# Batch 1's query pairs 2 and 3 transposed by DMA, and the third quarter of the output weights loaded earlier

## The chip, the cores and the metric

The kernel runs on one core of a Trainium2 chip. A core has a matrix engine (PE, with its weight loads listed apart as PEld), a vector engine (DVE), a scalar engine (ACT), a general engine (POOL), a queue engine that issues transfers (SP), and 16 DMA engines. Each engine runs its own instructions in order and waits on semaphores for the others. The metric is the device time in microseconds (us); lower is better. All times below are us unless they are marked ns.

## The reference

Two stages follow each other: a linear attention over 8 batches of 8 heads, 576 tokens and 64 channels a head, and a gated MLP whose input is the attention's output with the heads side by side (4608 tokens by 512 channels).

```python
q_s = exp(q - max(q)); q_s = q_s / sum(q_s, axis=-1)      # softmax of q over the channels
k_s = exp(k - max(k)); k_s = k_s / sum(k_s, axis=2)       # softmax of k over the tokens
kv  = einsum('bhsd,bhse->bhde', k_s, v)                   # 64 x 64 for each head
x   = einsum('bhsd,bhde->bhse', q_s, kv)                  # attention output, 4608 x 512 in all
h   = x @ w_in                                            # 512 -> 2048
out = (h * sigmoid(beta * h)) @ w_out                     # 2048 -> 512, float32
```

## The kernel before

**Tiles.** The tokens are worked off in nine slabs of 512 columns: slab t (0 to 7) holds the first 512 tokens of batch t, slab 8 the last 64 tokens of all eight batches. The heads go in four pairs `hp`, a pair filling 128 rows. For a slab, *pass 1* multiplies the slab's `XT` with `WIN` into `GT` (16 tiles `f` of 128 features, four products each) and ACT applies the gate; *pass 2* multiplies `GT` with `WOUT` (16 features by four token groups `u`, 64 products) into four PSUM banks, which are copied to `O2S` and stored.

**What a batch needs before its slab.** `load_swapped` brings q into `QF` in four pieces `x` (256 KB each): piece 0 has pair 0, piece 1 pair 2, and pieces 2 and 3 together pairs 1 and 3. `load_k` and `load_v` bring `KF` and `VF`. `exp_q` (L309, instruction L314, on ACT) makes `EQ`; `norm_main` (L331) normalises it: a row sum (L338) and a reciprocal (L339) on DVE, and a product (L340) on DVE or POOL. The normalised `EQ` must be turned so that the channels lie on the rows, into `QT`. There are two ways: `t_steps` (L375) turns 128 x 128 blocks on PE against an identity (L370, PSUM) and copies them out with one instruction for a group of pairs (L391), and `t_dma` (L396) lets a transfer, issued on SP, do it (L401). `exp_kc` (L318, instruction L322) makes `EK` on ACT, `cast_v` (L352, instruction L357) makes `VB`. `kv_half` multiplies `VB` and `EK` of two pairs on PE and normalises the result on DVE into `KVC` (L441, L443); `out_half` multiplies `QT` and `KVC` and copies the result to `XT` (L459), one pair by ACT and one by DVE.

**The order of the work** is written out by hand: the program is one list of operations, each engine gets its own in list order, and waits follow from the tiles that are read and written. Transfers are nearly all issued on SP, also in list order, so one that has to wait holds back those that stand behind it. What batch 1 needs is put between the products of slab 0's pass 2: the function `tick` counts products (the count starts at 64 there, as pass 1 of slab 0 stands ahead), and a list `todo` (L754) says at which count which steps of batch 1 are put in. Pairs 0 and 1 go first (`kv_half(1, (7, 0), 0)`, `out_half(1, (1, 2), 0)`), pairs 2 and 3 follow after pass 2 (L814, L817), between the first products of slab 1's pass 1 (`by_m`).

**Weights.** `w_out` comes in five loads (`load_wout`, L550) into staging tiles that `w_in` used before: features 0 to 3, 4 to 7, 8 to 11 (1 MB each), 12 and 13, then 14 and 15 one by one. `scale_wout` (L560, instruction L562 on DVE) multiplies each feature's 128 x 512 by 1/beta and writes `WOUT`; pass 2 needs feature f's `WOUT` for its products 4f+1 to 4f+4, except that for the last two features the order is by halves of the token groups. In the list the load of features 8 to 11 stands behind q's pieces 0, 2 and 3 of batch 1, and the loads of batch 2 (`load(2)`) stand ahead of all of these DVE and ACT steps.

Of the kernel before, what the change touches and what calls it, by code (L numbers as in the profile page):

```python
# [163 lines left out]
def bass_efficient_attn_shen__then__act_swish_beta_kernel(  # L164
# [12 lines left out]
    with ExitStack() as es:  # L177
# [94 lines left out]
        def load_swapped(b, xs=range(4)):  # L272
            i = b % 2
            for x in xs:
                s0, d0, n = SLOTS[x]
                a = bass.AP(qt_h, (b * H + s0) * S * D,
                            [[4 * D, 128], [n * S * D, 2], [1, 4 * D]])
                o = bass.AP(QF[i], d0 * 4 * D, [[H * 4 * D, 128], [n * 4 * D, 2], [1, 4 * D]])
                add(SP, lambda e, o=o, a=a: e.dma_start(o, a),
                    w=[("qf", i, hp, x) for hp in ((0,), (2,), (1, 3), (1, 3))[x]],  # L280
                    slot=f"qs{i}{x}")
# [70 lines left out]
        def cast_v(b, hp, eng=POOL, part=None):  # L352
            i = b % 2
            j0, n = ((0, NG), (0, 5), (5, 4))[0 if part is None else part + 1]
            o = bass.AP(VB[i], (hp * NG + j0) * VW, [[NHP * NG * VW, 128], [VW, n], [1, 64]])
            a = bass.AP(VF[i], hp * KW + j0 * D, [[NHP * KW, 128], [64, n], [1, 64]])
            add(eng, lambda e: (e.copy if eng == ACTE else e.tensor_copy)(o, a),  # L357
                r=[("vf", i, hp), ("vone", i)],
                w=[("vb", i, hp, h) for h in ((0, 1) if part is None else (part,))])
# [15 lines left out]
        def t_steps(b, hps, pool=MB, eng=DVE):  # L375
            i = b % 2
            st = {}

            def one(n, hp, j):
                if n == 0 and j == 0:  # L380
                    st["b"] = bank(pool)
                p = PS[st["b"]]
                pb = p[:, :].bitcast(BF16)
                c = n * 512 + j * 128
                mm(pb[:, c:c + 128], bass.AP(EQ[i], hp * 512 + j * 128, [[2048, 128], [1, 128]]),
                   IDB[:, :], True, True, r=[("eq", i, hp), "idb"], w=[("ps", st["b"])],
                   bk=st["b"], tr=True)
                if n == len(hps) - 1 and j == 3:
                    w = len(hps) * 512
                    o = bass.AP(QT[i], hps[0] * 512, [[2048, 128], [1, w]])  # L390
                    add(eng, lambda e: (e.copy if eng == ACTE else e.tensor_copy)(o, pb[:, 0:w]),  # L391
                        r=[("ps", st["b"])], w=[("qt", i, h) for h in hps], bank=[st["b"]])
            return [lambda n=n, hp=hp, j=j: one(n, hp, j) for n, hp in enumerate(hps)
                    for j in range(4)]
# [146 lines left out]
        def go(steps):  # L541
            for s in steps:
                s()
# [16 lines left out]
        def scale_wout(f, n=4):  # L560
            for f in range(f, f + n):
                add(DVE, lambda e, f=f: e.tensor_scalar(  # L562
                    WOUT[:, f, :], STAGE[f // 4][:, f % 4, :], RB[:, f:f + 1], None, ALU.mult),
                    r=[SKEY[f // 4][f % 4], "rb"], w=[("wout", f)])
# [122 lines left out]
                at(m)  # L687
        load_wout(0)
        load_wout(4)
        load_swapped(1, (0, 2, 3))  # L690
        load_wout(8)
        load_swapped(1, (1,))
        load_k(1, 4, (0, 1))
        load_wout(12, 2)
        load_v(1, 4, (0, 1))
# [51 lines left out]
        for t in range(NSLAB):  # L747
            todo = []
            if t == 0:
                def evacs():  # L750
                    o2_evac(0, 0, 3, DVE)
                    o2_evac(0, 1, 4, ACTE)

                todo = [(104, lambda: go(t_steps(1, (0, 1), (1,), ACTE))),  # L754
                        (104.1, lambda: cast_v(1, 0, ACTE)),
                        (111, lambda: go(t_steps(1, (2, 3), (2,), ACTE))),
                        (111.1, lambda: (scale_wout(14, 2), exp_kc(1, 2), exp_kc(1, 3))),
                        (116, lambda: kv_half(1, (7, 0), 0)),
                        (122, lambda: out_half(1, (1, 2), 0)), (124.5, evacs)]
            elif t == 1:  # L760
                todo = [(103, lambda: (kv_prods(2, (1, 2), (0, 2)), kv_evac(2, (1, 2)))),
                        (118, lambda: block(2))]
            elif t < 7:
                todo = [(104, lambda: block(t + 1))]
            todo = sorted(todo, key=lambda x: -x[0])
            slot = [0]

            def tick():
                slot[0] += 1
                while todo and todo[-1][0] <= slot[0]:  # L770
                    todo.pop()[1]()

            if 2 <= t < 7:
                if t < 5:
                    load(t + 2 if t == 2 else t + 3)
                for hp in (0, 2):
                    norm_main(t + 1, hp, 2)
                    t_dma(t + 1, hp, 2)
                if t in (2, 3, 4, 6):
                    norm_rem(t // 2 if t != 3 else 0)  # L780
                    tr_dma(t // 2 if t != 3 else 0)
                if t == 2:
                    load(5)
            elif t == 1:
                for hp in range(NHP):
                    cast_v(2, hp)
            if t < 2:
                slot[0] = NM * FIRST[t]
            for f in range(FIRST[t] if t < 2 else 0, NF):
                pass1_tile(t, f, tick)  # L790
            if t == 0:
                load(2)
                scale_wout(0)
                scale_wout(4)
                exp_q(1, (0, 1, 3, 2))
                norm_main(1, 0, 1, POOL)
                norm_main(1, 1, 1, POOL)
                norm_main(1, 3, 1, POOL)
                scale_wout(8)
                norm_main(1, 2, 1, POOL)  # L800
                exp_kc(1, 0, 2)
                scale_wout(12, 2)
                for hp in range(1, NHP):
                    cast_v(1, hp)
                pass2_group(0, (0, 1, 2, 3), (3, 4, 5, 6), tick)
                while todo:
                    todo.pop()[1]()
                at = by_m(1, 0, FIRST[1])
                o2_evac(0, 2, 5, ACTE)
                o2_evac(0, 3, 6, DVE)  # L810
                add(ACTE, lambda e: e.activation(DUMMY[:, 2:3], WARM[:, 0:1], ACT.Silu),
                    r=["warm"], w=["dummy"])
                at(0, 0, 3)
                kv_half(1, (7, 0), 2)  # L814
                at(1, 0, 3)
                at(0, 3, 5)
                out_half(1, (7, 7, 7, 0), 2)  # L817
                at(0, 5)
                at(1, 3)
                at(2)  # L820
                at(3)
                store(0)
                load(3)
                load_qrem(0)
                continue
            nb = [t + 2] if t + 2 < B else []
            if t == 1:
                nb = [2, 3]
            late = []
            for b in nb:  # L830
                if t == 1 and b == 2:
                    exp_q(2)
                    for hp in range(2):
                        norm_main(2, hp, 1, POOL)
                    t_dma(2, 0, 2)
                for hp in (0, 2):
                    exp_kc(b, hp, 2)
                if b > 2:
                    late.append(b)
                if b > 3:  # L840
                    for hp in range(NHP):
                        cast_v(b, hp)
            for b in late:
                exp_q(b)
                if b % 2 == 1:
                    exp_qr(b // 2)
                if b == 3:
                    exp_qr(0)
            for u in range(4):
                if (t, u) == (8, 3):  # L850
                    last_tile(u, ((0, 384), (384, 512)), (OB[orot[0] % 2], MB[0]))
                    continue
                pass2_group(t, (u,), (OB[orot[0] % 2],), tick)
                orot[0] += 1
                if t == 1 and u == 0:
                    for hp in range(2, 4):
                        norm_main(2, hp, 1, POOL if hp == 2 else DVE)
                    t_dma(2, 2, 2)
                    for hp in range(NHP):
                        cast_v(3, hp)  # L860
            while todo:
                todo.pop()[1]()
            if t < 8:
                store(t)
# [30 lines left out]
```

The softmax here doesn't subtract the row's maximum and nothing guards it: scores larger than these inputs give would overflow.

## Time and profile before

| | |
|---|---|
| median of 9 runs | 280.04 us (279.42 to 281.3) |
| the profiled execution | 279.77 us, its span 278.0 us |
| PE busy | 273.0 us, 98% of the span |
| ACT, DVE, POOL busy | 166.5, 103.0 and 35.2 us |
| DMA, mean rate | 180 GB/s, 50.12 MB in all |
| granted TensorE clock | 1.0 over the whole span |

The page gives one execution's span from its first to its last instruction; the time that is measured is 1.77 us longer (279.77 against 278.0). A group line of the page names the source line, the engine, the operation and the tiles (written <- read), how many there were, their busy time and the mean of one, and behind the bar how long the engine had been idle just before them, and who ended that. A line of the timeline gives the start, the length, the engine and queue (SPq is SP's issuing), the source line and how many instructions were drawn together. Matrix products overlap: the next one starts 0.216 us after the last while one is listed as 0.379 us long, so a run of n products reads n x 0.216 plus 0.16.

### The profile page before, as it was taken

The page shows a single profiled execution, that of the slowest core. Times are in us where ns is not written, and L with a number is a line of the kernel's source. Part 1 is how long each engine was busy: PE and PEld are TensorE (multiplying, and loading weights), DVE is VectorE, ACT ScalarE, POOL GpSimd, SP SyncE. Part 2 cuts the span into 40 slices and gives each one's busy share as a digit, 9 for nine tenths or more (in the row PEclk, how much of TensorE's full clock was granted, in tenths as well). Part 3 has the DMA queues.
Part 4 walks back from the last instruction along what each step waited for, and adds up shares of the span by engine and source line. Part 5 has one row for each costly group of instructions (what it writes and reads, how often), then busy time and mean ns, then how long its engine had stood idle before and what let it go on. Part 6 is the DMA issues. An engine that isn't in the chain of part 4 may idle for free.

```text
span 278.0 us, 4625 instructions
## 1 busy us (share of the span) xinstructions
PE 273.0 (98%) x1929; PEld 131.4 (47%) x1929; DVE 103.0 (37%) x204; ACT 166.5 (60%) x240; POOL 35.2 (13%) x52
## 2 busy tenths in 40 slices
PE   7999999999999999999999999999999999999995
PEld 3545444444445454545454545444444444444443
DVE  4744785007580149115720562035603200110012
ACT  5768666899578736793579447953741275027500
POOL 2630341308000305030003000000000000000000
PEclk9999999999999999999999999999999999999999
DMA  7999999999099998950599133002500110011022
GB/s 234 381 387 401 386 390 374 400 377 152 6 324 338 232 358 258 388 109 2 170 387 201 21 151 75 2 4 110 136 0 2 75 75 2 0 81 70 2 74 77
DMA packets 42173, 50.12 MB, mean 180 GB/s; under 512 B 21028, under 2 KB 29476, under 8 KB 41000
## 3 DMA queue, kind: packets, MB, share of 16 engines
q1 hardware_dynamic: 41312, 48.90, 55.0%
q10 hardware_dynamic: 840, 0.93, 1.0%
q8 instruction: 15, 0.25, 0.4%
q14 instruction: 6, 0.05, 0.1%
HBM read 36.71 MB, written 9.44 MB: 166 GB/s over the span
## 4 chain that ended last, share of the span: by engine, by line
PE 86%; DMA 8%; SPq 4%; DVE 1%; issue 0%
PE PS L372 86%; DMA O2S<-in_moe_w_out_dram 4%; DMA O2S<-in_moe_w_in_dram 4%; SPq L569 2%; SPq L250 1%; DVE WOUT L562 1%; SPq L293 0%; PE PS L370 0%; SPq L298 0%; DVE O2S L724 0%
## 5 line engine op out<-in xcount | busy, mean ns | idle before, releaser
L648 ACT ACTIVATE GT<-PS,BETA 128x512 bf16<-128x512 f32 x144 | 96.4, 690 | 61.5 <-PE PS L372 61.4
L372 PE MATMUL PS<-WOUT,GT 128*128 128x512 bf16 (+2 forms) x592 | 128.0, 374 | 0.1
L372 PE MATMUL PS<-XT,WIN 128*128 128x512 bf16 x576 | 126.3, 379 | 0.0
L372 PEld LDWEIGHTS PS<-XT,WIN 128*128 128x128 bf16 x576 | 60.4, 105 | 63.3 <-issue 0.7
L372 PEld LDWEIGHTS PS<-WOUT,GT 128*128 128x128 bf16 x592 | 56.4, 98 | 66.5 <-DVE WOUT L562 1.1
L703 DVE COPY O2S<-PS 128x512 f32<-128x512 f32 x33 | 22.7, 688 | 124.6 <-PE PS L372 124.5
L357 POOL CAST VB<-VF 128x576 bf16<-128x576 f32 x29 | 20.7, 714 | 85.3 <-DMA VF<-in_v_dram 84.1
L338 DVE TENSOR_REDUCE QS<-EQ 128x8 f32<-128x512 bf16 (+1 forms) x22 | 20.1, 912 | 17.6 <-ACT EQ L314 17.6
L459 ACT CAST XT<-PS 128x512 bf16<-128x512 f32 x14 | 7.6, 587 | 23.1 <-PE PS L372 23.1
L322 ACT ACTIVATE EK<-KF 128x1152 bf16<-128x1152 f32 (+1 forms) x19 | 18.4, 1005 | 4.1 <-DMA KF<-in_k_dram 3.9
L314 ACT ACTIVATE EQ<-QF 128x512 bf16<-128x512 f32 x32 | 17.7, 616 | 3.1 <-DMA QF<-in_q_dram 3.1
L340 DVE TENSOR_TENSOR EQ<-EQ,QI 128x1024 bf16<-128x1024 bf16 (+1 forms) x12 | 14.3, 1192 | 0.4
L340 POOL TENSOR_TENSOR EQ<-EQ,QI 128x512 bf16<-128x512 bf16 x10 | 10.5, 1048 | 30.4 <-DVE QI L339 30.1
L459 DVE CAST XT<-PS 128x512 bf16<-128x512 f32 x14 | 9.1, 686 | 12.8 <-PE PS L372 12.8
L372 PEld LDWEIGHTS PS<-VB,EK 64*64 64x64 bf16 x576 | 6.5, 107 | 4.5 <-issue 2.5
L372 PE MATMUL PS<-VB,EK 64*64 64x65 bf16 x576 | 7.9, 193 | 0.3 <-POOL VB L357 0.3
L648 ACT ACT_TABLE_LOAD x5 | 6.4, 1283 | 0.1
L372 PE MATMUL PS<-XT 128*128 128x512 f32 x6 | 5.0, 1009 | 1.5 <-DVE XT L226 1.5
L372 PE MATMUL PS<-QT,KVC 64*64 64x512 bf16 x64 | 6.2, 384 | 0.1
L562 DVE TENSOR_SCALAR WOUT<-O2S,RB 128x512 bf16<-128x512 f32 x8 | 5.3, 703 | 0.8 <-DMA O2S<-in_moe_w_out_dram 0.6
L339 DVE RECIPROCAL QI<-QS 128x8 f32<-128x8 f32 (+1 forms) x22 | 5.0, 226 | 0.8
L322 ACT ACT_TABLE_LOAD x4 | 5.1, 1283 | 0.1
(51 smaller groups left out, 68.6 us busy)
## 6 DMA issues: line engine op xcount, KB each, us to landing
out_dram<-O2S SPq DMA_DIRECT2D x8, 1024.0 KB, 4.5
QF<-in_q_dram SPq DMA_DIRECT2D x30, 256.0 KB, 5.9
KF<-in_k_dram SPq DMA_DIRECT2D x6, 1152.0 KB, 8.3
VF<-in_v_dram SPq DMA_DIRECT2D x6, 1152.0 KB, 11.3
KF<-in_k_dram SPq DMA_DIRECT2D x8, 288.0 KB, 8.2
VF<-in_v_dram SPq DMA_DIRECT2D x8, 288.0 KB, 8.5
WST<-in_moe_w_in_dram SPq DMA_DIRECT2D x8, 256.0 KB, 7.5
O2S<-in_moe_w_in_dram SPq DMA_DIRECT2D x4, 512.0 KB, 11.0
```

Source lines behind the costliest of these rows:

```text
L314: add(ACTE, lambda e, o=o, a=a: e.activation(o, a, ACT.Exp), r=[("qf", i, hp, x) for x in ((2, 3) if hp % 2 else (hp // 2,))], w=[("eq", i ...
L322: add(ACTE, lambda e: e.activation(o, a, ACT.Exp), r=[("kf", i, h) for h in range(hp, hp + n)], w=[("ekc", i, h) for h in range(hp, hp + n)])
L338: add(DVE, lambda e: e.tensor_reduce(s_, a, AX.X, ALU.add), r=ks, w=[("qs", i, hp0)])
L339: add(DVE, lambda e: e.reciprocal(v_, s_), r=[("qs", i, hp0)], w=[("qi", i, hp0)])
L340: add(eng, lambda e: e.tensor_tensor(a, a, vb, ALU.mult), r=ks + [("qi", i, hp0)], w=ks)
L357: add(eng, lambda e: (e.copy if eng == ACTE else e.tensor_copy)(o, a), r=[("vf", i, hp), ("vone", i)], w=[("vb", i, hp, h) for h in ((0, 1 ...
L372: add(PE, lambda e: e.matmul(o, l, r_, start=start, stop=stop, tile_position=tp), r=r, w=w, bank=[bk])
L459: add(eng, lambda e, eng=eng, bk=bk, hp=hp: (e.copy if eng == ACTE else e.tensor_copy)(XT[i][:, hp, :], PS[bk][:, :]), r=[("ps", bk)], w=[ ...
L562: add(DVE, lambda e, f=f: e.tensor_scalar(WOUT[:, f, :], STAGE[f // 4][:, f % 4, :], RB[:, f:f + 1], None, ALU.mult), r=[SKEY[f // 4][f % ...
L569: add(SP, lambda e: e.dma_start(STAGE[c][:, m:m + nm, :], a), w=SKEY[c][m:m + nm], slot=f"win{c}{m}")
L648: add(ACTE, lambda e: e.activation(GT[:, f, :], PS[bk][:, :], ACT.Silu, scale=BETA[:, f:f + 1]), r=[("ps", bk), "beta"], w=[("gt", f)], ba ...
L703: add(eng, lambda e: (e.copy if eng == ACTE else e.tensor_copy)(O2S[t % 2][:, u, :], PS[bk][:, :]), r=[("ps", bk)], w=[("o2", t % 2, u)], ...
```

## The change

Four things are moved in the list, all of them for slab 0's pass 2.

1. q's piece 3 of batch 1 is loaded behind the 1 MB of output weights 8 to 11, not ahead of it.
2. On DVE the four `scale_wout(8)` stand ahead of the normalisation of pairs 1 and 3, not behind it; the normalisation of pair 2 stands behind features 12 and 13, and its product is done by DVE, not by POOL.
3. Pairs 2 and 3 of batch 1 are turned by `t_dma`, not on PE: eight PE turns and one ACT copy go, one SP transfer comes. It stands on SP behind the last of batch 1's values, and `load(2)` stands behind it.
4. The PE turns of pairs 0 and 1 stand three products later (count 107, not 104); `exp_kc` of pairs 2 and 3 stands at count 119.1, not 111.1, with the same neighbours on ACT.

```diff
         load_wout(0)
         load_wout(4)
-        load_swapped(1, (0, 2, 3))
+        load_swapped(1, (0, 2))
         load_wout(8)
-        load_swapped(1, (1,))
+        load_swapped(1, (3, 1))
         load_k(1, 4, (0, 1))
...
-                todo = [(104, lambda: go(t_steps(1, (0, 1), (1,), ACTE))),
-                        (104.1, lambda: cast_v(1, 0, ACTE)),
-                        (111, lambda: go(t_steps(1, (2, 3), (2,), ACTE))),
-                        (111.1, lambda: (scale_wout(14, 2), exp_kc(1, 2), exp_kc(1, 3))),
+                todo = [(107, lambda: go(t_steps(1, (0, 1), (1,), ACTE))),
+                        (107.1, lambda: cast_v(1, 0, ACTE)),
+                        (111.1, lambda: scale_wout(14, 2)), (119.1, lambda: (exp_kc(1, 2), exp_kc(1, 3))),
                         (116, lambda: kv_half(1, (7, 0), 0)),
                         (122, lambda: out_half(1, (1, 2), 0)), (124.5, evacs)]
...
             if t == 0:
-                load(2)
                 scale_wout(0)
                 scale_wout(4)
                 exp_q(1, (0, 1, 3, 2))
                 norm_main(1, 0, 1, POOL)
+                scale_wout(8)
                 norm_main(1, 1, 1, POOL)
                 norm_main(1, 3, 1, POOL)
-                scale_wout(8)
-                norm_main(1, 2, 1, POOL)
                 exp_kc(1, 0, 2)
                 scale_wout(12, 2)
+                norm_main(1, 2, 1)
+                t_dma(1, 2, 2)
+                load(2)
                 for hp in range(1, NHP):
                     cast_v(1, hp)
```

## The prediction

> **What bounds the kernel now.** I read the page's busy line and its chain first, then the chain in order of time, then each engine's timeline around slab 0's pass 2 (28 to 47 us), last DMA from 33 to 72 us.
>
> ```profile
> PE 273.0 (98%) x1929; PEld 131.4 (47%) x1929; DVE 103.0 (37%) x204; ACT 166.5 (60%) x240; POOL 35.2 (13%) x52
> ```
> ```profile
> 22.63 11.78 DMA O2S<-in_moe_w_out_dram
> 34.40 0.03 issue
> 34.43 1.79 DVE WOUT L562 x2
> 36.22 0.05 issue
> 36.27 1.04 PE PS L372 x4
> 37.30 0.45 PE PS L370 x8
> 37.75 1.51 PE PS L372 x7
> 39.26 0.45 PE PS L370 x8
> 39.71 235.30 PE PS L372 x1667
> ```
>
> PE is the bound: from 39.71 on the chain is PE alone, to 275 us. Ahead of that it runs through the load of weights 8 to 11 (lands 34.40) and two scalings. So what PE loses or saves before 39.71 moves the end one for one, unless a later wait eats it, and a new PE wait anywhere is paid in full.
>
> ```profile
> 29.81 1.67 DVE L562 TENSOR_SCALAR WOUT<-WST,RB 128x512 bf16<-128x512 f32 x4 [1.02 <-DMA WST<-in_moe_w_out_dram]
> 34.43 2.58 DVE L562 TENSOR_SCALAR WOUT<-O2S,RB 128x512 bf16<-128x512 f32 x4
> 37.93 1.77 DVE L562 TENSOR_SCALAR WOUT<-O2S,RB 128x512 bf16<-128x512 f32 x2
> 40.79 0.49 DVE L562 TENSOR_SCALAR WOUT<-O2S,RB 128x512 bf16<-128x512 f32 x1 [0.19 <-DMA O2S<-in_moe_w_out_dram]
> 41.78 0.23 DVE L443 TENSOR_TENSOR KVC<-PS,RC 128x64 bf16<-128x64 f32 x1
> ```
> ```profile
> 33.70 2.22 POOL L340 TENSOR_TENSOR EQ<-EQ,QI 128x512 bf16<-128x512 bf16 x2 [0.27 <-DVE QI L339]
> 39.48 0.74 POOL L357 CAST VB<-VF 128x576 bf16<-128x576 f32 x1 [0.46 <-DMA VF<-in_v_dram]
> ```
> ```profile
> 28.07 9.24 PE L372 MATMUL PS<-WOUT,GT 128*128 128x512 bf16 x40
> ```
>
> Four scalings take 1.67 alone but 2.58 beside POOL's products; two take 1.77 beside one. PE's 40 products need 40 x 0.216 + 0.16 = 8.80 and take 9.24: 0.44 is waiting for those scalings.
>
> **The change, part by part.**
>
> *Weights 8 to 11.* One 256 KB piece of q no longer stands ahead: at the 374 GB/s of that slice 0.70, so they land at 33.70, not 34.40 (the issue stays at 22.63, as it waits there for its staging tile). The four scalings run 33.73 to 35.40 with POOL idle (its product of pair 0 is over at 33.44). PE wants feature 8 at 28.07 + 32 x 0.216 = 34.98 and feature 9 at 35.84: both are ready. Saved: 0.44.
>
> *PE turns of pairs 2 and 3.* Eight turns take 0.45 of PE's order (39.26 to 39.71). Saved: 0.45, together 0.89. The ACT copy (1.01) goes as well; ACT has idle time there and this is worth nothing.
>
> *What is late next, POOL.* `kv_half` needs `VB` of pair 1, whose values land at 39.43; POOL's cast ends at 40.22, unchanged. PE would come to it at 28.07 + 52 x 0.216 + 0.45 = 39.75 and waits to about 40.27; today it starts at 40.72. The 0.89 is capped at 0.45.
>
> *What is late next, DVE.* q's piece 3 lands at 33.70 + 0.70 = 34.40, so ACT's pair 1 (0.63 each) is done at 35.11 and pair 3 at 35.63; pair 2 is unchanged. DVE then does pair 1's sum and reciprocal (0.69 + 0.20, with 0.03 between) after the scalings: 35.32 to 36.2, pair 3's to 37.0. POOL's products (1.04 each) run 36.37 to 37.41 and 37.49 to 38.53. PE turns pair 1 at 28.07 + 43 x 0.216 + 0.22 = 37.58: just in time. Features 12 and 13 (landed at 37.9) meet POOL's second product: the first scaling ends about 0.28 after it, as it does today, at 38.8, the second at 39.2; PE wants feature 12 at 38.89, just in time. Pair 2's sum and reciprocal follow to 40.04, its product on DVE takes 0.63 (half of the 128x1024 one's 1.22 to 1.23) and meets the cast of `VB`, so 40.7. Features 14 and 15 then end at 41.5 instead of 41.28, and the four KVC instructions, 0.77 in all, at 42.25 instead of 42.01. `out_half` starts on PE about 0.13 after its KVC, at 42.38; today it starts at 42.53. Of the 0.45 only 0.15 is left. Bounds: nothing (the product takes 0.98, as it does at 65.74 beside a POOL product) and 0.45 (DVE is not late); I take 0.15, from the durations above.
>
> The Trainium skill, "SBUF — State Buffer", on port sharing, says that a DVE product with two SBUF inputs and a POOL instruction block each other outright, whoever starts second. By that pair 2's product would wait to 40.22 and end at 40.85, and the gain would be nearer 0.0 than 0.15; the row's 0.98 says much the same.
>
> *The turn by DMA.*
>
> ```profile
> 32.89 0.43 SPq L250 DMA_DIRECT2D VF<-in_v_dram  x1
> 33.37 5.53 SPq L279 DMA_DIRECT2D QF<-in_q_dram  x4
> 40.35 1.26 SPq L250 DMA_DIRECT2D VF<-in_v_dram  x1
> 53.25 12.23 SPq L261 DMA_DIRECT2D QRF<-in_q_dram  x16
> 65.52 2.68 SPq L401 DMA_TRANSPOSE QT<-EQ  x2
> ```
>
> SP waits for both products (POOL 38.53, DVE 40.7), issues at 40.75 and is free at 42.0. The last values issued at 32.89 land 10.9 later, at 43.8, and the turn stands behind them. Its price is taken from the turns issued at 80.83 and 87.19, which landed 10.7 and 5.3 later (91.5 and 92.5) right after values that landed at 90.6: 0.9 to 1.0 each. So `QT` of pairs 2 and 3 is there at 44.8. PE wants it at 46.52 - 0.15 = 46.37. Cover 1.5. Bounds: 0.9 as above, and 3.1, the least time from issue to landing of any turn, if nothing of that overlaps (46.9: PE waits 0.5). I take 1.0.
>
> *Everything behind it on SP.* `load(2)` is issued from 42.0, not 33.37. Transfers issued before it last to 43.8 and the turn to 44.8, so DMA does not run dry; but all that follows lands 1.0 later. Batch 2's values land at 53.6 instead of 52.6, PE wants their products at 67.47: hidden. Batch 3's keys land at 62.1 and values at 66.1; ACT takes the keys from 65.4 and POOL the values from 66.3: hidden. The 16 remainder pieces of q (12.23 of SP) move as well, and so do batch 2's two turns, 65.52 to 66.5. Today the second, issued at 66.97, is listed as landed 4.9 later, at 71.84, and PE uses it at 72.44 (its second group of four, 0.22 into this):
>
> ```profile
> 72.22 0.62 PE L372 MATMUL PS<-QT,KVC 64*64 64x512 bf16 x8
> ```
>
> That is 0.6 of slack against a shift of 1.0. But 15 of its 16 parts landed by 70.34; the last one stood behind a 16 KB instruction fetch (packet at 69.85, 0.96 long). PE's 15 fetches come about every 257 of its instructions; 16 fewer (turns with their weight loads) put this one 8 products or 1.7 later, at 71.4, after the turn. Then it lands at 71.34 and PE wants it at 72.29: 0.95 of cover. This is the point on which the forecast hangs.
>
> The Trainium skill, "DMA: Bandwidth & Descriptors", in its anatomy of one DMA, speaks against this part: any semaphore wait is served by the issuing sequencer before dispatch. A turn that waits for arithmetic holds the whole queue behind it; by the rule alone the 8.7 from 33.37 to 42.0 is lost, by the rows the backlog to 43.8 hides all of it.
>
> **The sum.** -0.89 + 0.44 (values) + 0.30 (DVE) + 0 (both turns) = -0.15. The profiled execution took 279.77 with a span of 278.0, and is 0.27 under the median of 280.04. 280.04 - 0.15 = 279.9.
>
> **The rivals.**
> - *Batch 2's second turn is late* (slower). For it: no more than 0.6 to 0.95 of cover, and the turn's DMA time inside a stream of loads is not in the trace. Against it: the fetch should have moved, and DMA stands still from 70 to 72. It decides from a shift of 1.95, or of 1.45 if the fetch (1.0) hits again: at a shift of 2.0 with the fetch PE waits 1.0 to 1.5 less the 0.15: 280.9, with 281.4 at a shift of 2.5.
> - *Batch 1's turn is late.* From 2.5 after the last values on, PE waits at 46.4: at 3.1 about 0.5 there, and then the shift of 3.1 brings the first rival's wait too: 281.3.
> - *DVE is not late*: 280.04 - 0.45 = 279.6.
> - *The weights do not land earlier*, if the load's own issue and not the piece of q ahead sets it. The scalings then run 34.43 to 36.1, uncontended; feature 9 is ready at 35.4, and the cap by `VB` is the same; DVE is 0.7 later throughout, which costs about 0.5 at `out_half`: 280.4.
>
> **How the numbers follow.** Forecast 0.52 (279.9); DVE not late 0.12 (279.6); weights not earlier 0.08 (280.4); batch 2's turn late 0.20 (280.4 to 281.4); batch 1's turn late 0.08 (281.3). What this kernel's measurement can tell from no change is about 0.3%, 0.84 us. Under 279.2 no case reaches, only the spread of the measurement (0.04). Over 280.88 are half of the fourth case, all of the fifth and a little for what I don't see: 0.22. The rest, 0.74, is within. The range, 279.3 to 281.2, leaves out the ends of the last two cases.
>
> **What would show it.** Weights 8 to 11 scaled from 33.7 in about 1.67; no gap in PE up to `kv_half`, then one of about 0.5 for `VB`; `out_half` at 42.4; the new transfer issued at 40.7, landed by 45; SP's remainder loads 1.0 later; batch 2's second turn landed before 72.3. I am wrong if PE waits at 46.4 or 72.3, or if the shift behind the turn is over 1.5.

## The result, and the profile after

The changed kernel takes 285.03 us (median of 10 runs, 281.39 to 286.23) where the kernel before takes 280.01 (31 runs beside it): a ratio of 1.0125, 95% interval 1.0098 to 1.0152. By that ratio it is slower by 1.25%. Two of the ten executions took 281.39 and 281.61 at a mean clock of 1.0 and the other eight 284.17 to 286.23 at 0.988 to 0.994; ratios, here and below, leave out executions more than 1.5% above their kernel's fastest (four of these ten, from 285.62 up, and two of the hold alone), so this one is below the 1.018 of the two medians. The profiled execution took 284.17 us, its span 282.4, against 279.77 and 278.0 before: 4.4 more to explain.

The page's busy line of the changed kernel, and PE's table of waits (engine, line, whom it waited for, the sum, how often, the longest):

```profile
PE 274.8 (97%) x1921; PEld 131.7 (47%) x1921; DVE 101.8 (36%) x205; ACT 165.7 (59%) x239; POOL 33.7 (12%) x51
```
```profile
PE PS L372 <- DMA QT<-EQ: 2.9, 2, 2.5
PE PS L372 <- DVE XT L226: 1.5, 1, 1.5
PE PS L372 <- POOL VB L357: 0.2, 1, 0.2
```

The first wait is new: twice, 2.9 in all, PE waits for a turn by DMA. The other two stood before with 1.5 and 0.3. PE's timeline tells which turn it is. First slab 0's pass 2 and the start of slab 1:

```profile
28.18 9.44 PE L372 MATMUL PS<-WOUT,GT 128*128 128x512 bf16 x43
...
39.95 0.75 PE L372 MATMUL PS<-VB,EK 64*64 64x65 bf16 x36
...
42.03 0.67 PE L372 MATMUL PS<-QT,KVC 64*64 64x512 bf16 x4
...
46.64 12.26 PE L372 MATMUL PS<-XT,WIN 128*128 128x512 bf16 x56
```

and the last two of these lines in the kernel before:

```profile
42.53 0.41 PE L372 MATMUL PS<-QT,KVC 64*64 64x512 bf16 x4
...
46.86 12.26 PE L372 MATMUL PS<-XT,WIN 128*128 128x512 bf16 x56
```

Here the change does what it should. 43 products run in 43 x 0.216 + 0.16 = 9.44, without the gap of 0.44; the PE turns of pairs 2 and 3 are gone (eight turns of pairs 0 and 1 are left, at 37.46); and the batch that was turned by DMA is not waited for: pass 1 of slab 1 runs from 46.64, where it ran from 46.86. That is a gain of 0.22. Then batch 2's two groups of QT products in slab 1's pass 2, in the changed kernel (the last line of such a timeline goes on past the stretch that was asked for, so of it only the start is read):

```profile
72.64 0.41 PE L372 MATMUL PS<-QT,KVC 64*64 64x512 bf16 x4 [0.44 <-DMA QT<-EQ]
75.54 0.64 PE L372 MATMUL PS<-QT,KVC 64*64 64x512 bf16 x4 [2.50 <-DMA QT<-EQ]
76.11 3.42 PE L372 MATMUL PS<-WOUT,GT 128*128 128x512 bf16 x10
79.37 3.83 PE L372 MATMUL PS<-XT,WIN 128*128 128x512 bf16 x17
```

and what followed the eight products at 72.22 in the kernel before:

```profile
72.78 2.33 PE L372 MATMUL PS<-WOUT,GT 128*128 128x512 bf16 x10
74.95 5.34 PE L372 MATMUL PS<-XT,WIN 128*128 128x512 bf16 x24
```

The second group starts at 75.54 instead of 72.44 (0.22 into the eight), and the ten products behind it take 3.42 instead of 2.33. From the second group to slab 2's pass 1 it is 3.83 instead of 2.51. So the ledger is: -0.22 from slab 0, +3.32 for the two waits (from 0.22 early to 3.10 late), +1.32 for slow products: +4.42, which is the whole difference. The slow products are the clock's; stretches of the changed kernel (busy time and, in brackets, instructions of PE, PEld, DVE, ACT and POOL; granted clock; the share of the 16 DMA engines that is busy; GB/s):

```profile
74.00:76.00 2.00, 0.46 (x4) 0.13 (x4) 0.00 (x0) 0.00 (x0) 0.00 (x0) 0.73 0.00 0
76.00:78.00 2.00, 2.00 (x9) 0.74 (x6) 1.42 (x5) 1.73 (x2) 0.00 (x0) 0.50 0.00 0
```

The clock falls within the long wait and stands at 0.50 for the two microseconds behind it (0.91 in the next two); before, it was 1.0 in all of them.

Why the turn is late is on SP's timeline of the changed kernel, and in the stretches around the new turn, first of the changed kernel, then of the kernel before:

```profile
33.21 0.43 SPq L250 DMA_DIRECT2D VF<-in_v_dram  x1
40.85 1.34 SPq L401 DMA_TRANSPOSE QT<-EQ  x1
42.24 2.12 SPq L279 DMA_DIRECT2D QF<-in_q_dram  x4
...
55.93 11.91 SPq L261 DMA_DIRECT2D QRF<-in_q_dram  x16
67.88 4.20 SPq L401 DMA_TRANSPOSE QT<-EQ  x2
```
```profile
40.00:42.00 2.00, 1.94 (x43) 0.92 (x42) 1.91 (x7) 0.42 (x1) 0.17 (x1) 1.00 0.89 330
42.00:44.00 2.00, 2.00 (x12) 0.81 (x11) 1.51 (x3) 1.30 (x3) 0.95 (x2) 1.00 1.18 174
44.00:46.00 2.00, 2.00 (x45) 0.89 (x43) 1.38 (x5) 1.98 (x4) 0.40 (x1) 1.00 0.97 305
```
```profile
40.00:42.00 2.00, 2.00 (x44) 0.95 (x43) 1.62 (x6) 1.22 (x2) 0.22 (x1) 1.00 1.05 384
42.00:44.00 2.00, 2.00 (x13) 0.75 (x12) 1.03 (x3) 1.19 (x3) 0.78 (x2) 1.00 1.10 357
44.00:46.00 2.00, 2.00 (x45) 0.94 (x44) 1.44 (x6) 1.98 (x4) 0.55 (x1) 1.00 1.09 366
```

The turn is issued at 40.85 and `load(2)` from 42.24. DMA moves 330, 174 and 305 GB/s in these three stretches, where it moved 384, 357 and 366 before. Engines without work are only part of that: the busy share falls to 0.89 between 40 and 42 (0.41 from 41.5 to 42), but between 42 and 44 it is 1.18, so there the engines are busy and move little. Batch 2's values land at 55.26 (before 52.63), batch 3's at 67.69 (65.21), the remainder loads of q are issued 55.93 to 67.84 (53.25 to 65.48), and batch 2's turns are issued at 67.88 and 70.68 and land at 72.59 and 75.50 (before 69.42 and 71.84). The shift is 2.5, not 1.0.

### The profile page after: what moved, and what is told of

Same layout as the page of the kernel before. It is cut to its first block, busy times and chain, and to the rows that moved or that the text cites. A ratio compares the mean times of both kernels' runs of the same rounds, so it can differ in the third digit from the quotient of the medians.

```text
span 282.4 us, 4609 instructions
## 1 busy us (share of the span) xinstructions
PE 274.8 (97%) x1921; PEld 131.7 (47%) x1921; DVE 101.8 (36%) x205; ACT 165.7 (59%) x239; POOL 33.7 (12%) x51
## 3 DMA queue, kind: packets, MB, share of 16 engines
HBM read 36.71 MB, written 9.44 MB: 163 GB/s over the span
## 4 chain that ended last, share of the span: by engine, by line
PE 72%; DMA 17%; SPq 7%; POOL 1%; DVE 1%; issue 1%; POOLq 0%
PE PS L372 72%; DMA VF<-in_v_dram 5%; DMA WST<-in_moe_w_out_dram 4%; DMA O2S<-in_moe_w_out_dram 4%; SPq L250 3%; DMA WST<-in_moe_w_in_dram 2%; SPq L279 2%; DMA QT<-EQ 2%; POOL VB L357 1%; POOL WIN L573 1%; SPq L401 1%; DVE WOUT L562 0%; SPq L293 0%; DVE EQ L340 0%; SPq L569 0%
## 5 line engine op out<-in xcount | busy, mean ns | idle before, releaser
L340 POOL TENSOR_TENSOR EQ<-EQ,QI 128x512 bf16<-128x512 bf16 x9 | 9.4, 1043 | 28.8 <-DVE QI L339 28.5
L372 PE MATMUL PS<-QT,KVC 64*64 64x512 bf16 x64 | 6.9, 401 | 2.9 <-DMA QT<-EQ 2.9
L562 DVE TENSOR_SCALAR WOUT<-O2S,RB 128x512 bf16<-128x512 f32 x8 | 3.8, 526 | 2.3 <-DMA O2S<-in_moe_w_out_dram 2.3
```

What stands on the lines that cost most here:

```text
L340: add(eng, lambda e: e.tensor_tensor(a, a, vb, ALU.mult), r=ks + [("qi", i, hp0)], w=ks)
L372: add(PE, lambda e: e.matmul(o, l, r_, start=start, stop=stop, tile_position=tp), r=r, w=w, bank=[bk])
```

## What is to be told apart

The ledger says where the time is lost. Three things are left to show. **A**: the loss is that of batch 2's second turn, made late by a shift of the stream of transfers, and not something in slab 0. **A1** says that the shift comes from the hold (batch 2's loads stand on SP behind a turn that waits for arithmetic, and the DMA engines run out of work); its rival is that the turn itself, as a transfer in the stream, makes it. **C**: the last 1.3 is the clock's, and follows from PE's standing still.

## The experiments

### The new order without the turn and the hold

The changed kernel with the PE turns of pairs 2 and 3 back, the product by POOL again, and `load(2)` in its old place:

```diff
-                        (111.1, lambda: scale_wout(14, 2)), (119.1, lambda: (exp_kc(1, 2), exp_kc(1, 3))),
+                        (114, lambda: go(t_steps(1, (2, 3), (2,), ACTE))),
+                        (114.1, lambda: (scale_wout(14, 2), exp_kc(1, 2), exp_kc(1, 3))),
...
             if t == 0:
+                load(2)
                 scale_wout(0)
...
+                norm_main(1, 2, 1, POOL)
                 exp_kc(1, 0, 2)
                 scale_wout(12, 2)
-                norm_main(1, 2, 1)
-                t_dma(1, 2, 2)
-                load(2)
```

> The new order of loads and scalings alone; pairs 2 and 3 of batch 1 turned on PE again, and batch 2's loads back in their old place. Theory A (all of the loss comes from the turn by DMA standing on SP ahead of batch 2's loads): 279.5 to 279.9, a gain of 0.1 to 0.5 over before, and no PE wait at 72. Rival R (the new order is to blame, wholly or in part): over 281.

Measured: 280.13, ratio 1.0009 (0.9997 to 1.0022). DMA moves 370 GB/s between 41 and 47, as it did before, batch 2's values land at 53.06 in an execution whose pass 2 began 0.23 later, and PE does not wait for a turn. So the new places of weights 8 to 11, of their scalings and of q's piece 3 cost nothing (pair 2's normalisation stands ahead of features 12 and 13 here, not behind them as in the changed kernel). They also gain nothing by themselves: PE waits 0.29 for POOL's product of pair 2 at 40.28, so the gain of 0.2 isn't to be had from this part alone.

### The turn and its hold without the new order

The kernel before, with the turn in place of the PE turns and `load(2)` behind it:

```diff
-                        (111, lambda: go(t_steps(1, (2, 3), (2,), ACTE))),
...
-                load(2)
                 scale_wout(0)
...
                 norm_main(1, 2, 1, POOL)
+                t_dma(1, 2, 2)
+                load(2)
                 exp_kc(1, 0, 2)
```

> The kernel before with the turn of pairs 2 and 3 by DMA, batch 2's loads behind it on SP; the order of weights and scalings is the old one, and the turn can be issued at about 39.1, 1.7 earlier than in the changed kernel, as POOL has the product done by then. Theory A: PE waits for batch 2's turns at 72 again, 281 to 285. Rival R: 279.5 to 280.3, no such wait.

Measured: 280.71, ratio 1.0026 (1.0014 to 1.0039). The turn is issued at 39.03 and lands at 45.02; the values of batch 2 land at 55.55, and batch 2's second turn at 73.83. On this kernel's PE timeline:

```profile
72.42 0.41 PE L372 MATMUL PS<-QT,KVC 64*64 64x512 bf16 x4
73.87 0.41 PE L372 MATMUL PS<-QT,KVC 64*64 64x512 bf16 x4 [1.04 <-DMA QT<-EQ]
74.44 2.11 PE L372 MATMUL PS<-WOUT,GT 128*128 128x512 bf16 x9 [0.16 <-issue]
```

The wait is that of the changed kernel, but 1.04 long, and the clock stays at 1.0: the products behind it keep their 0.216. The place of the wait was foretold, its size was not; the kernel is slower by 0.7, not by 5.

### The hold alone

The first experiment's kernel (PE turns, no turn by DMA for batch 1), with `load(2)` issued only when the last operation of `kv_half` on pairs 0 and 1 is done (`load` gets that operation as an argument):

```diff
-                        (116, lambda: kv_half(1, (7, 0), 0)),
+                        (116, lambda: kv_half(1, (7, 0), 0)), (116.1, lambda: load(2, P.ops[-1])),
...
-                load(2)
                 scale_wout(0)
```

> The first kernel with batch 2's loads held back on SP to about 42.2, as in the changed kernel, but no turn by DMA. Theory A1 (the hold makes the shift: DMA engines that have no work left by 41.5 stand still until the loads come): batch 2's values land 1.2 to 2.0 later than before (53.8 to 54.6), PE waits up to 1 at 72, 279.9 to 281.5. Theory A2 (the turn's own time in the DMA queue makes it): the values land less than 0.5 later, no PE wait, 279.5 to 279.9.

Measured: 281.12 (280.01 to 285.86), ratio 1.0036 (1.0016 to 1.0056); the profiled execution took 280.56. `load(2)` is issued from 41.64; one of its stretches and its second QT group:

```profile
42.00:44.00 2.00, 2.00 (x13) 0.72 (x11) 1.03 (x3) 1.27 (x3) 0.95 (x2) 1.00 0.74 214
```
```profile
73.34 0.41 PE L372 MATMUL PS<-QT,KVC 64*64 64x512 bf16 x4 [0.62 <-DMA QT<-EQ]
```

Batch 2's values land at 55.15: 2.5 later than before, more than the 1.2 to 2.0 expected, without any new turn. A hold to 41.6 is enough for the shift, though the last transfer issued ahead of it landed at 43.66. That landing is the last of the 16 parts of the transfer; half of them had landed by 42.06, and their engines had nothing behind (share 0.74 between 42 and 44, against 1.10 before).

### The remainder loads behind batch 2's turns

The changed kernel, with the eight remainder loads of q that stand ahead of batch 2's turns on SP moved behind the second one, so that the turns are issued earlier and the stream stays as late as it is:

```diff
-                load_qrem(0)
...
-                if b == 3:
+                if b == 4:
                     exp_qr(0)
...
                     t_dma(2, 2, 2)
+                    load_qrem(0)
```

> The changed kernel with eight of the sixteen remainder loads of q moved behind batch 2's second turn on SP (and the ACT step that reads them moved one slab later). Theory A (the turns are late because SP and the DMA queue reach them late): the turns are issued at about 66.7 and land by 71, PE does not wait at 72 and keeps its full clock, 279.6 to 280.0, although batch 2's values still land at about 55. Rival (the turns are slow by themselves, wherever they stand): PE still waits 1 or more, over 281.5.

Measured: 286.92, ratio 1.0253 (1.0232 to 1.0275). The edit brought a wait of its own: moved to the next slab, `exp_qr(0)` stood behind loads of later batches into the same tile, which leaves the remainder tokens of batches 0 and 1 to be computed from the q of batches 4 and 5, and ACT waited 12.37 for that tile and PE 5.12 behind it, at 110. At the place in dispute there was no wait: the second turn landed at 73.39, and PE did its eight products in one piece from 73.08 on, in 0.76 instead of 0.62. The edit was made again with the later load behind `exp_qr(0)`:

```diff
-            if b % 2:
+            if b % 2 and b != 5:
                 load_qrem(b - 1)
...
+                if b == 4:
                     exp_qr(0)
+                    load_qrem(4)
```

> The changed kernel with eight of the sixteen remainder loads of q behind batch 2's second turn, and this time the loads that reuse their tile (batches 4 and 5) stand behind the ACT step that reads it. Theory A (the turns are late because SP and the DMA queue reach them late): the second turn lands by 73.4 at the latest (as it did in the run before, where PE passed this place without a wait), PE loses at most 0.7 there and keeps its full clock, 279.6 to 280.5, although batch 2's values still land at about 55. Rival (the turns are slow by themselves): PE waits 1 or more there, over 281.5.

Measured: 279.67, ratio 0.9994 (0.9982 to 1.0007). From SP's and PE's timelines of this kernel:

```profile
65.03 3.78 SPq L401 DMA_TRANSPOSE QT<-EQ  x2
```
```profile
46.81 12.26 PE L372 MATMUL PS<-XT,WIN 128*128 128x512 bf16 x56
...
72.17 0.62 PE L372 MATMUL PS<-QT,KVC 64*64 64x512 bf16 x8
72.73 2.33 PE L372 MATMUL PS<-WOUT,GT 128*128 128x512 bf16 x10
74.90 5.34 PE L372 MATMUL PS<-XT,WIN 128*128 128x512 bf16 x24
```

The values of batch 2 still land at 55.45, so the shift is there; but the turns land at 71.74 and 72.20, no group waits, the clock is 1.0, and the loss of 1.25% is gone. A is shown: all that the change costs is paid at this one turn.

### Work for PE in the long wait

The changed kernel with 11 products of zeros (`warm`, into a bank that the real products overwrite) between batch 2's two groups:

```diff
             for a in halves:
+                if (b, a) == (2, 2):
+                    warm(11, bks[2])
                 for hp, ro, co in quad(a):
```

> The changed kernel with eleven products of zeros (2.4 us of PE) between the first and the second group of batch 2's QT products, where PE waits for the second turn; they write a PSUM bank that the second group then overwrites. Theory C (the half clock after the wait comes from PE standing idle for 2.5): the clock stays at 1.0 over the whole span in nearly all executions; those that waited longest gain 1.3, those that waited shortly lose up to 1.5: all between 282.3 and 283.5. Rival (the clock falls for another reason): it falls here too, and the median stays at 284.5 or more.

Measured: 283.22 (282.25 to 283.45), ratio 1.0099 (1.0075 to 1.0124). The four executions lie between 282.25 and 283.45, where the changed kernel's spread over 281.39 to 286.23, and the intervals of the two ratios overlap, so the time alone decides little. PE's timeline:

```profile
72.96 2.55 PE L372 MATMUL PS<-WARM 128*128 128x512 bf16 x11
75.98 0.41 PE L372 MATMUL PS<-QT,KVC 64*64 64x512 bf16 x4 [0.47 <-DMA QT<-EQ]
76.32 2.33 PE L372 MATMUL PS<-WOUT,GT 128*128 128x512 bf16 x10
78.49 3.83 PE L372 MATMUL PS<-XT,WIN 128*128 128x512 bf16 x17
```

The turn is as late as in the changed kernel (it landed at 75.94), but with PE busy the ten products take 2.33 again, and from the second group to pass 1 it is 2.51, not 3.83. The second group starts 0.44 later than in the changed kernel, and 1.32 less 0.44 is the 0.9 between the two profiled executions, 283.27 and 284.17. C is shown for the profiled execution: 1.32 of its loss is the half clock after an idle PE.

### The turn in ACT's queue

If the hold is the cause, the turn could go in a queue that holds nothing. The changed kernel with that turn issued by ACT and `load(2)` in its old place; and the same with the remainder loads moved as in the experiment before last (its two diffs, repaired form):

```diff
-            add(SP, lambda e: e.dma_start_transpose(o, a), r=[("eq", i, hp) for hp in hps],
+            add(eng, lambda e: e.dma_start_transpose(o, a), r=[("eq", i, hp) for hp in hps],
...
-                        (111.1, lambda: scale_wout(14, 2)), (119.1, lambda: (exp_kc(1, 2), exp_kc(1, 3))),
+                        (111.1, lambda: scale_wout(14, 2)), (119.1, lambda: (t_dma(1, 2, 2, ACTE), exp_kc(1, 2), exp_kc(1, 3))),
...
+                load(2)
                 scale_wout(0)
...
-                t_dma(1, 2, 2)
-                load(2)
```

> The changed kernel with the turn of pairs 2 and 3 issued by ACT in its own queue, ahead of exp_kc of pair 2, and batch 2's loads back ahead of all that waits on SP. Theory A1 (the hold on SP makes the shift): batch 2's values land at most 1.0 later than before (53.6), the second turn of batch 2 by 72.8, no or a short PE wait, 279.6 to 280.3. Rival A2 (the turn's own DMA time makes the shift): the values land 2.0 or more later, 281 or more.

> Both of these: the turn issued by ACT, and eight remainder loads behind batch 2's second turn. Theory A: PE has no wait at 72 whatever the turn costs in the DMA queue, and the saving at pass 2 of slab 0 (0.2 to 0.3) is kept: 279.5 to 279.9. Rival (the saving is an artefact of one execution): 280.0 or more.

Measured: 291.54, ratio 1.0407 (1.0383 to 1.0431), and 291.30, ratio 1.0396 (1.0375 to 1.0416). Both theories are missed by 11. The rivals' signs are there, values of batch 2 more than 2.0 later (58.75 and 56.07) and times over 281 and 280, but neither foresaw such a price. From the first one's PE timeline:

```profile
56.72 0.64 PE L372 MATMUL PS<-QT,KVC 64*64 64x512 bf16 x4 [9.54 <-DMA QT<-EQ]
57.30 14.30 PE L372 MATMUL PS<-XT,WIN 128*128 128x512 bf16 x56
```

The turn was issued at 41.56 and landed at 56.68, 15.1 later, where the one behind the loads on SP landed 3.8 after its issue; batch 2's keys, issued at 39.59, landed at 54.23. Beside a queue that is never empty the turn advanced only with the loads, and the loads with it: the turn's 1024 packets, now on a queue of their own, start between 45.88 and 55.81, and batch 2's values landed at 58.75 instead of 52.63.

### Loads ahead of the turn

If the hold makes the shift, giving the DMA engines some of batch 2's loads ahead of the turn takes it away in steps. The changed kernel with the first one, `(0,)`, or the first two, `(0, 1)`, of batch 2's four q pieces ahead (`load` gets the rest as an argument):

```diff
                 norm_main(1, 2, 1)
+                load_swapped(2, (0, 1))
                 t_dma(1, 2, 2)
-                load(2)
+                load(2, (2, 3))
```

> The changed kernel with the first of batch 2's four q pieces issued ahead of the turn. Theory (the hold of the loads makes the shift): that piece fills about 0.7 of the hole of 2.5 in the DMA stream, so batch 2's values land at 54.5 instead of 55.3, the turn at about 45.4 instead of 44.6 (PE wants it at 46.3: no wait), PE waits 0.7 to 1.7 for batch 2's second turn, and the time is 280.5 to 282.5. Rival (the DMA time of the turn makes the shift): values still at 55.3, time 284 to 286 as in the changed kernel.

> The same with two pieces ahead of the turn. Theory: 1.4 of the hole is filled, values of batch 2 at 53.9, the turn at 46.1, just ahead of PE; batch 2's second turn is waited for by 0.5 or less and the time is 279.7 to 280.7. Rival: values at 55.3 and 284 to 286; or the turn lands after 46.3 and PE waits there by as much.

Measured: 280.64, ratio 1.0015 (1.0002 to 1.0029), and 280.88, ratio 1.0025 (1.0013 to 1.0037). The times fell within the first theory's ranges or close by, but its mechanism did not show: the values of batch 2 land at 55.07 and 54.96, hardly earlier than the changed kernel's 55.26. The stream stays 2.3 to 2.4 late although the DMA engines have work. With two pieces ahead, DMA moves

```profile
42.00:44.00 2.00, 2.00 (x11) 0.71 (x9) 1.39 (x4) 1.23 (x4) 0.99 (x2) 1.00 1.54 278
44.00:46.00 2.00, 1.80 (x43) 0.89 (x43) 1.29 (x5) 1.98 (x4) 0.35 (x1) 1.00 0.81 208
```

at most 278 GB/s for four microseconds around a turn that is 0.26 MB. So the rival has a case too, and it got a run of its own.

### A turn that nobody waits for

The kernel before, with one turn more, of batch 0's pairs 2 and 3 into a tile that nothing reads, ahead of `load(2)`. Its source is written long before, so it waits for no arithmetic:

```diff
+        def t_extra():
+            o = bass.AP(QX, 0, [[2 * SM, 128], [128, 8], [1, 128]])
+            a = bass.AP(EQ[0], 2 * SM, [[NHP * SM, 128], [1, 2 * SM]])
+            add(SP, lambda e: e.dma_start_transpose(o, a), r=[("eq", 0, 2), ("eq", 0, 3)],
+                w=["qx"], slot="trx")
...
+                t_extra()
                 load(2)
```

> The kernel before with one more turn by DMA, of batch 0's pairs 2 and 3 into a tile that nothing reads, right ahead of batch 2's loads on SP: its source is long written, so SP holds nothing, and only the turn's own place in the stream of loads is priced. Theory L (a turn also makes the 16 engines level up, so that the lead of the faster ones is lost): batch 2's keys and values land 1.5 to 2.5 later (values at 54.1 to 55.1 instead of 52.6), the 16 parts of the turn and of the piece ahead of it land within 0.3 of each other, PE waits 0.3 to 1.5 for batch 2's second turn, and the time is 280.3 to 281.2. Theory O (a turn costs its own 0.9 and no more, as the forecast had it): values at 53.5, no PE wait, 279.9 to 280.2.

Measured: 281.05, ratio 1.0037 (1.0021 to 1.0053). From its SP and PE timelines (line numbers are 1 to 7 higher in this kernel) and its stretch:

```profile
33.16 7.17 SPq L408 DMA_TRANSPOSE QX<-EQ  x1
40.38 2.48 SPq L280 DMA_DIRECT2D QF<-in_q_dram  x4
```
```profile
73.55 0.41 PE L373 MATMUL PS<-QT,KVC 64*64 64x512 bf16 x4 [0.31 <-DMA QT<-EQ]
```
```profile
42.00:44.00 2.00, 2.00 (x12) 0.71 (x11) 1.00 (x4) 1.28 (x3) 0.87 (x2) 1.00 1.03 150
```

SP is held after all, for 7.17 by the turn's own issue, but the loads behind it come at 40.38, and DMA doesn't run out of work: the share between 42 and 44 is 1.03, where the hold alone left 0.74, and yet it moves only 150 GB/s. Theory L holds. The 16 parts of each transfer, as the trace has their landings (first, middle and last of the 16):

```
                   before              extra turn          hold alone          changed kernel
b.1 keys, last     41.05 41.50 43.01   41.05 41.52 42.92   41.09 41.35 42.94   41.20 41.36 42.93
b.1 values, last   41.95 42.38 43.83   43.60 43.67 43.75   41.82 42.06 43.66   41.91 42.13 43.67
new turn                               44.50 44.56 44.62                       44.48 44.55 44.62
b.2 q, piece 1     42.71 43.11 44.56   45.30 45.35 45.40   43.79 44.19 44.51   45.30 45.36 45.41
b.2 q, piece 4     44.95 45.33 46.81   47.55 47.57 47.61   46.30 46.74 48.17   47.45 47.61 48.37
b.2 keys           47.96 48.35 49.80   50.55 50.61 52.09   49.33 50.41 52.28   50.40 50.59 52.06
b.2 values         50.94 51.37 52.63   53.54 53.60 55.16   52.90 53.58 55.15   53.73 54.37 55.26
```

Read the middle column of each kernel. The DMA engines do not work in step: before, the middle one is 1.3 to 1.5 ahead of the last throughout. A turn ends that lead. Ahead of it the values' parts land together (43.60 to 43.75), then the turn's, then piece 1's: by the last part the turn cost 0.87, by the middle one 44.56 - 42.38 = 2.2. The packets in the trace show how. The turn goes in 1024 packets of 256 bytes, most of them 0.02 long; but 19 of the first ones start between 41.76 and 43.24, as one engine after the other gets to the turn, and all end between 43.51 and 43.55, 0.33 after the last engine has finished the values (43.18). In the changed kernel 19 such packets end between 43.52 and 43.57, 0.33 after 43.19. So the engines that are ahead stand in the turn's first packets until the last one has reached it; the trace doesn't name the engine of a packet, so this is read from the times.

Some microseconds later one part falls back again (50.66 against 52.09 for keys; a 16 KB packet of instructions, 1.12 long, stands at 49.32), and then the landings, too, are 2.5 late. The hold does the same by another way: the engines that lead have nothing to do. In 40 to 50 us the trace has 3.78 MB moved before, 3.25 with the extra turn (0.26 of it the turn's own), 3.03 with the hold alone, 3.14 with both (0.26 the turn's): the loads lose 0.79, 0.75 and 0.90 MB, at 378 GB/s 2.1, 2.0 and 2.4 us. Either cause is enough, and the two together cost little more than one, since both waste the same lead. A1 was half of it.

### Loads ahead and remainder loads behind

Two pieces ahead of the turn, and the remainder loads behind batch 2's second one (with the repair of the experiment above, not shown again), as a version that might beat both kernels:

```diff
+                load_swapped(2, (0, 1))
                 t_dma(1, 2, 2)
-                load(2)
+                load(2, (2, 3))
...
-                load_qrem(0)
...
                     t_dma(2, 2, 2)
+                    load_qrem(0)
```

> Two pieces ahead of the turn, and the eight remainder loads of batches 0 and 1 behind batch 2's second turn. Theory: no PE wait at 46 nor at 72, and what is left of the change is its gain of 0.2 in slab 0's second pass: 279.5 to 279.9 against 280.0, a ratio of 0.998 to 1.000. Rival: the gain is eaten elsewhere, 280.0 or above.

Measured: 280.01, ratio 0.9990 (0.9978 to 1.0003). Its PE timeline has neither wait:

```profile
46.80 0.41 PE L372 MATMUL PS<-QT,KVC 64*64 64x512 bf16 x4
...
72.63 0.62 PE L372 MATMUL PS<-QT,KVC 64*64 64x512 bf16 x8
```

The ratio leaves room for the gain of 0.2 in slab 0 and doesn't prove it. No version here is measurably faster than the kernel before.

## Why the prediction was wrong

By its own steps:

- *Weights 8 to 11, DVE, POOL, the sum of slab 0.* Right. On DVE and POOL of the changed kernel:

```profile
33.73 1.67 DVE L562 TENSOR_SCALAR WOUT<-O2S,RB 128x512 bf16<-128x512 f32 x4 [1.40 <-DMA O2S<-in_moe_w_out_dram]
40.08 0.69 DVE L340 TENSOR_TENSOR EQ<-EQ,QI 128x512 bf16<-128x512 bf16 x1
```
```profile
36.38 2.17 POOL L340 TENSOR_TENSOR EQ<-EQ,QI 128x512 bf16<-128x512 bf16 x2 [2.92 <-DVE QI L339]
39.50 0.67 POOL L357 CAST VB<-VF 128x576 bf16<-128x576 f32 x1 [0.96 <-DMA VF<-in_v_dram]
```

  The scalings begin at 33.73, as foretold to the hundredth. DVE's product beside the cast of `VB` took 0.69, between the 0.63 taken and the row's 0.98; the two stood beside each other for only 0.09, so this says little about how they get on. `out_half` began at 42.03, where 42.38 was foretold and 42.53 stood before, but its four products took 0.67 instead of 0.41, waiting inside; behind them 0.24 was left, at the second one 0.22. Forecast -0.15, measured -0.22.
- *The turn by DMA.* Right for what it was asked: issued at 40.85 (40.75), landed at 44.62 (44.8), not waited for.
- *Everything behind it on SP.* This is the step that failed: "DMA does not run dry; but all that follows lands 1.0 later". Measured 2.5. Two errors stand behind it. The cover up to 43.8 was a landing, that is the last of 16 parts; the engines that were ahead ran out of work from about 41.5 on, and the turn's packets start at 42.12. And the turn's price, 0.9 to 1.0, was again taken from last parts, in rows where the values landed just ahead of it. In the trace of before those values' parts landed between 90.47 and 90.57 while the keys ahead of them had spread from 86.31 to 87.60, and 21 packets of the turn behind them, begun between 89.28 and 89.67, all ended between 90.39 and 90.44: the levelling stood there to be read. The forecast held that a turn's DMA time inside a stream of loads is not in the trace; its packets are.
- *Batch 2's second turn, and the fetch.* The forecast moved the 16 KB packet of instructions out of the way, to 71.4. In the changed kernel such packets stand at 68.58 and at 73.34, the second 1.12 long; the one that stood at 69.85 came earlier, not later, and why is not shown. Of the turn's 16 parts 15 landed by 73.88 and the last at 75.50. That the packet made this last 1.6 is argued from the times, not shown. Without that part and the half clock that followed, the profiled execution would stand, by estimate, at 284.17 - 1.6 - 1.3 = 281.3, near the 281.39 and 281.61 of the two at full clock, of which there is no trace.
- *The rivals.* The first one is what happened, at the point it named ("decides from a shift of 1.95"); at a shift of 2.5 it gave 281.4. The kernels whose wait stayed at 0.3 to 1.3 (turn alone, hold alone, pieces ahead, extra turn) lie at 280.6 to 281.1. It had no term for the clock: a wait of 2.9 in two pieces cost 1.32 more. The Trainium skill, "DMA: Bandwidth & Descriptors", in its anatomy of one DMA, has a wait served on the issuing sequencer before dispatch. What the forecast took from this, that a waiting turn holds all that stands behind it, was set aside because of the backlog to 43.8; of the 8.7 of that hold the hold alone gives about a quarter, 2.0 to 2.5.

The chance of that rival, 0.20, was set too low: between the shift that the forecast took (1.0) and the point from which it turns (1.45 to 1.95) lay less than one microsecond, and the shift's price had come from two rows alone.

## What to carry to other kernels

Don't read the cover that a DMA backlog gives from landing times: a landing is that of the slowest of 16 engines, and what counts for the stream is when the middle one runs out of work. Price a turn by DMA that stands between loads by the bytes that the stream moves less around it, here 2.1 us for 0.26 MB, not by its own issue and landing. And when a wait of PE grows towards three microseconds, add the products at half clock behind it: 1.32 here after waits of 0.44 and 2.50, nothing after single waits up to 1.26.

## What the runs showed of the hardware

- *A turn levels the DMA engines.* The parts of the transfer ahead of it landed within 0.15, where they spread over 1.9 without it, as the engines that were ahead stood in the turn's first packets, for up to 1.77, until the last one came. The Trainium skill, "Advanced Engine Details and Errata", on the X-bar transpose, says that transposing transfers on this chip are as fast as plain ones. By the last part this nearly holds: 0.87 against 0.74 for a q piece of the same 0.26 MB. By the bytes of the stream it does not: the loads lost 2.1.
- *A turn's issue can hold SP by itself.* Behind the loads that were still to land the extra turn took 7.17 to issue, though its source was ready; the four q pieces in its place took 5.53 before.
- *Half clock after a wait.* The clock was at 0.50 after waits of 0.44 and 2.50 with four short products between, and at 1.0 after single waits of 0.31 to 1.26. The Trainium skill, "TensorE: Matmul & The Clock Gate", under "What's actually happening", gives an idle window of about 3.4 us for that step. By the trace's record the clock was down from 74.94 to 78.35, 3.41 long, which agrees with that length; but it fell only 2.75 after the end of the VB products (71.36 + 0.83 = 72.19), and in the 3.41 ahead of the fall PE was busy for about 1.1. So a window that was not wholly idle was enough here, if the one that counts is the one right ahead of the fall.
- *Two queues are no way round.* A turn in ACT's queue beside SP's loads took 15.1 from issue to landing, against 3.8 behind fewer of them on SP, and made batch 2's values 6.1 late.

Open stays why the first of batch 2's turns takes 2.3 to 2.5 to issue in some kernels (the changed one, the turn alone, two pieces ahead) and 1.34 in others (before, one piece ahead, the extra turn), which moves the second turn by about 1; and why the loads of the changed kernel moved only 331 and 315 GB/s from 50 to 54 us, where the kernel with two pieces ahead moved 380 and 421.
